# A layernorm prologue with the first x chunk loaded as two column halves and its 1/std taken from ScalarE's square root

## The chip, the cores and the metric

The kernel runs on one core of one Trainium2 chip. The metric is device time in microseconds (us) of one execution; lower is better. Each version was run several times and once under the profiler.

The engines are TensorE (PE for matmuls, PEld for weight loads), VectorE (DVE), ScalarE (ACT), GpSimd (POOL) and SyncE (SP), which issues nearly all DMAs. A chunk is 128 tokens by 1024 columns; x has 16 of them, called x0 to x15.

## The reference, cut to what matters

```python
xn = layernorm(x)                              # x: 2048 tokens x 1024
y  = x + attention(xn, wq, wk, wv, wo, beta) + B(xn)

def B(x):                                      # a token-mixing MLP
    h = layernorm(x)                           # normalised a second time
    u = gelu(einsum('bsd,sf->bdf', h, w1) + b1)
    ...
```

Only the start of branch B matters for the change. The first matmul needs h of the first 128 tokens, so it needs mean and 1/std of chunk 0. Both layernorms of B are folded into one scale, with a constant `E_H` added to the variance. Everything after the first 35 us is the same in both kernels.

## The kernel before: the parts that matter

The prologue loads x and the first columns of w1 chunk by chunk on one queue. Even chunks have their statistics on VectorE, odd ones on ScalarE. The hidden matmuls consume a chunk as soon as its h and its w1 rows are there.

```python
# consts(): order of the loads, all issued by SyncE on one queue
for kind, c0, n in (("x", 0, 1), ("x", 1, 1), ("x", 2, 1), ("w", 0, 2), ("x", 3, 1), ("x", 4, 2),
                    ("w", 2, 2), ("x", 6, 2), ("w", 4, 4), ...):
    ...
# ten matmuls on zeros: TensorE has work while x0 is on its way
for _ in range(self.N_WARM):                   # N_WARM = 10
    fw.mm(self.bank(0), self.warm[:, 0:P], self.warm[:], start=True, stop=True)

# D, d  BN_STATS on VectorE (both halves / one half; d2' is the second half of chunk 2)
# A, A' sum, then sum of squares, on ScalarE
# S     add E_H (VectorE), then pow -0.5 (POOL)
# h     scale x into h (VectorE)
NORM_ORDER = (["D0 A1 S0 d2 h0 A1' A3 S1 d2' h1"] +
              [f"S{c} d{c + 2} h{c} A{c + 1}' A{c + 3} S{c + 1} d{c + 2}' h{c + 1}" for c in range(2, 14, 2)] +
              ["S14 h14 A15' S15 C h15"])

def early_hidden(self, c0, c1, bank_groups):   # per chunk: 8 matmuls of 512 columns
    for banks in bank_groups:                  # the first half of h, then the second
        reads = self.R_w1e[c0:c1] + ... + self.R_hh[banks[0] % 2][c0:c1]
        ...
```

Each engine runs its own words of `NORM_ORDER` in that order. A word that waits for data therefore holds up the words behind it on the same engine.

## Time and profile before

| | before |
|---|---|
| median of the runs beside the change | 697.27 us (696.95 to 698.75, 6 runs) |
| span of the profiled run | 695.2 us |
| PE busy | 685.3 us, 99% of the span |
| first matmul on real data | 6.83 us |
| x0, x1, x2, first w1 piece, x4 landed | 3.57, 4.23, 5.65, 6.55, 8.82 us |

Landings here and below are the last increment of each transfer's semaphore in the trace, in us from the start of the span. "x4" is the transfer that brings chunks 4 and 5.

From the page of the kernel before (busy time by engine; then the chain that ended last, by engine):

```profile
span 695.2 us, 11228 instructions
...
PE 685.3 (99%) x4746; PEld 326.5 (47%) x4830; DVE 257.2 (37%) x581; ACT 280.2 (40%) x333; POOL 100.1 (14%) x156
...
PE 98%; issue 1%; DMA 1%; DVE 0%; SPq 0%
...
```

The kernel is bound by TensorE from end to end. A change of the prologue can pay only by moving the whole stream of matmuls. What starts that stream is seen in the timeline of VectorE (start, duration, engine, line, operation, tiles; in brackets the idle time before it and what ended it):

```profile
...
3.60 1.42 DVE L617 BATCH_NORM_STATS2 ln_st<-xin 128x6 f32<-128x512 bf16 x2 [2.35 <-DMA xin<-in_A_x_dram]
5.05 0.21 DVE L620 BATCH_NORM_AGGREGATE ln_mv<-ln_st 128x2 f32<-128x12 f32 x1
5.29 0.15 DVE L639 TENSOR_SCALAR ln_mv<-ln_mv 128x1 f32<-128x1 f32 x1
5.67 0.69 DVE L617 BATCH_NORM_STATS2 ln_st<-xin 128x6 f32<-128x512 bf16 x1 [0.23 <-DMA xin<-in_A_x_dram]
6.29 0.72 DVE L656 TENSOR_SCALAR h<-xin,ln_mv,ln_rs 128x512 bf16<-128x512 bf16 x2
...
8.85 0.69 DVE L617 BATCH_NORM_STATS2 ln_st<-xin 128x6 f32<-128x512 bf16 x1 [0.28 <-DMA xin<-in_A_x_dram]
9.46 0.53 DVE L656 TENSOR_SCALAR h<-xin,ln_mv,ln_rs 128x1024 bf16<-128x1024 bf16 x1
...
```

The POOL pow runs from 5.53 to 6.08 us, between the third and the fifth of these lines. Then h0 is held until 6.29 by the statistics of chunk 2. The line at 8.85 is chunk 4's statistics, released by the landing of x4; h2 stands right behind it. TensorE's timeline shows one stream from 6.83 us on, with no gap:

```profile
...
1.25 4.06 PE L194 MATMUL ps_all<-warm 128*128 128x512 bf16 x10 [1.25 <-DVE brow L517]
6.83 9.44 PE L194 MATMUL ps_all<-h,w1early 128*128 128x512 bf16 x42 [1.51 <-DVE h L656]
```

### The profile page before, as it was taken

The numbers are of one execution on the slowest core, as the hardware profiler recorded it, in microseconds if no ns is written. First come the engines' busy times: TensorE is split into PE (matmuls) and PEld (weight loads), VectorE is DVE, ScalarE is ACT, GpSimd is POOL, SyncE is SP. The second block draws the span as 40 slices with busy tenths as digits, with TensorE's granted clock in tenths as the row PEclk, the third lists the DMA queues.
The fourth block names the chain that finished last, engine by engine and source line by source line (L and its number), as shares of the span: only waits on it lengthen the run. The fifth ranks groups of instructions, "written<-read, shape, count | busy, mean of one in ns | idle before, by whom it ended". The sixth has DMA issues, their size and how long they took to land.

```text
span 695.2 us, 11228 instructions
## 1 busy us (share of the span) xinstructions
PE 685.3 (99%) x4746; PEld 326.5 (47%) x4830; DVE 257.2 (37%) x581; ACT 280.2 (40%) x333; POOL 100.1 (14%) x156
## 2 busy tenths in 40 slices
PE   8999999999999999999999999999999999999998
PEld 3444444444444444444444454444444444445454
DVE  6740000000011334334436455536445553434445
ACT  7622222111134444444545444454544444534440
POOL 2600000000001111211121211112121111121130
DMA  9497685226045536645263544626273544436014
GB/s 315 110 221 175 149 227 124 74 60 140 1 138 116 111 65 133 117 107 124 49 126 97 118 95 88 129 47 137 66 148 80 97 95 73 98 63 151 9 31 137
DMA packets 210537, 77.17 MB, mean 111 GB/s; under 512 B 173112, under 2 KB 202808, under 8 KB 210488
## 3 DMA queue, kind: packets, MB, share of 16 engines
q1 hardware_dynamic: 210344, 76.42, 47.9%
q8 instruction: 38, 0.62, 0.4%
q14 instruction: 11, 0.09, 0.0%
q10 hardware_dynamic: 144, 0.03, 0.0%
HBM read 59.79 MB, written 5.24 MB: 94 GB/s over the span
## 4 chain that ended last, share of the span: by engine, by line
PE 98%; issue 1%; DMA 1%; DVE 0%; SPq 0%
PE ps_all L194 98%; DMA xin<-in_A_x_dram 1%; SPq L216 0%; DVE ln_st L617 0%; DVE h L656 0%; DVE fin L1050 0%; PE ps_all L200 0%
## 5 line engine op out<-in xcount | busy, mean ns | idle before, releaser
L194 PE MATMUL ps_all<-gT,w2h 128*128 128x512 bf16 x868 | 207.8, 380 | 1.6 <-issue 0.2
L810 ACT ACTIVATE pT<-ps_all 128x512 bf16<-128x512 f32 (+1 forms) x128 | 151.4, 1235 | 76.7 <-PE ps_all L194 76.7
L194 PE MATMUL ps_all<-h,w1s 128*128 128x512 bf16 x752 | 165.1, 379 | 0.8
L805 POOL TENSOR_SCALAR_AFFINE_SELECT pT<-pT 128x512 bf16<-128x512 bf16 x128 | 83.6, 677 | 557.3 <-ACT pT L810 557.3
L194 PEld LDWEIGHTS ps_all<-gT,w2h 128*128 128x128 bf16 x896 | 83.2, 98 | 105.6 <-issue 13.8
L194 PEld LDWEIGHTS ps_all<-h,w1s 128*128 128x128 bf16 x768 | 75.1, 98 | 90.6
L844 DVE CAST ost<-ps_all 128x264 bf16<-128x264 f32 (+1 forms) x128 | 49.2, 398 | 169.4 <-PE ps_all L194 169.4
L712 ACT ACTIVATE gT<-ps_all,b1c 128x512 bf16<-128x512 f32 x56 | 37.7, 689 | 138.4 <-PE ps_all L194 132.8
L754 DVE CAST kT<-ps_all 128x512 bf16<-128x512 f32 x32 | 22.0, 687 | 176.5 <-PE ps_all L194 176.5
L194 PE MATMUL ps_all<-xnT,wk 128*128 128x512 bf16 x256 | 60.5, 379 | 0.0
L194 PE MATMUL ps_all<-xnT,wq 128*128 128x512 bf16 x256 | 60.4, 378 | 0.0
L194 PEld LDWEIGHTS ps_all<-vA,pT 128*128 128x128 bf16 x1280 | 47.7, 96 | 22.7
L194 PE MATMUL ps_all<-wv_sb,xnT 128*128 128x512 bf16 x227 | 54.0, 379 | 1.6
L738 ACT ACTIVATE qT<-ps_all 128x512 bf16<-128x512 f32 x32 | 19.1, 597 | 78.4 <-PE ps_all L194 78.4
L194 PE MATMUL ps_all<-vA,pT 128*128 128x33 bf16 x1280 | 48.6, 177 | 0.0
L950 DVE SCALAR_TENSOR_TENSOR stg<-ps_all,b2c,stg 128x512 bf16<-128x512 f32 x32 | 24.0, 750 | 61.7 <-PE ps_all L194 61.6
L757 ACT ACTIVATE etmp<-kT 128x512 bf16<-128x512 bf16 x24 | 15.1, 629 | 59.0 <-DVE kT L754 59.0
L194 PEld LDWEIGHTS ps_all<-xnT,wk 128*128 128x128 bf16 x256 | 23.8, 98 | 23.1
L194 PEld LDWEIGHTS ps_all<-wv_sb,xnT 128*128 128x128 bf16 x256 | 23.5, 97 | 23.7
L194 PEld LDWEIGHTS ps_all<-xnT,wq 128*128 128x128 bf16 x256 | 23.4, 97 | 23.2
L772 ACT ACTIVATE vA<-ps_all 128x512 bf16<-128x512 f32 x32 | 19.2, 599 | 37.2 <-PE ps_all L194 37.2
L194 PE MATMUL ps_all<-qT,kT 32*128 32x384 bf16 (+3 forms) x512 | 31.9, 299 | 0.0
(70 smaller groups left out, 419.2 us busy)
## 6 DMA issues: line engine op xcount, KB each, us to landing
w2h<-in_B_w_dram SPq DMA_DIRECT2D x32, 448.0 KB, 4.8
w1s<-in_B_w_dram SPq DMA_DIRECT2D x12, 1024.0 KB, 5.7
wq<-in_A_wq_dram SPq DMA_DIRECT2D x32, 256.0 KB, 4.2
wk<-in_A_wk_dram SPq DMA_DIRECT2D x32, 256.0 KB, 5.0
stg<-in_A_x_dram SPq DMA_DIRECT2D x16, 256.0 KB, 2.9
out_dram<-stg SPq DMA_DIRECT2D x16, 256.0 KB, 2.0
xin<-in_A_x_dram SPq DMA_DIRECT2D x2, 1024.0 KB, 10.5
wv_sb<-in_A_wv_dram SPq DMA_DIRECT2D x2, 1024.0 KB, 8.7
```

What stands on the lines that cost most here:

```text
L194: ins = self.nc.tensor.matmul(*args, **kwargs)
L712: fw.op("act", lambda e: e.activation(self.gT[:, fc, half * 512:(half + 1) * 512], self.bank(b), ACT.Gelu_apprx_tanh, bias=self.b1c[:, fc: ...
L738: fw.op("act", lambda e: e.activation(self.qT[k][:], self.bank(b), ACT.Copy), reads=[self.R_bank[b]], writes=[self.R_qT[k]])
L754: fw.op("dve", lambda e: e.tensor_copy(self.kT[k][:], self.bank(b)), reads=[self.R_bank[b]], writes=[self.R_kT[k]])
L757: fw.op("act", lambda e: e.activation(self.etmp[1][:], self.kT[k][:], ACT.Exp), reads=[self.R_kT[k]], writes=[self.R_etmp[1]])
L772: fw.op("act", lambda e: e.activation(self.vA[i][:, c, :, 0:D_HEAD], self.bank(b).rearrange("p (h d) -> p h d", d=D_HEAD), ACT.Copy), read ...
L805: fw.op("pool", lambda e: e.affine_select(d, d, pattern=[[0, 4], [1, P]], compare_op=ALU.is_ge, fill=0.0, base=0, channel_multiplier=-1), ...
L810: self.fw.op("act", lambda e: e.activation(dst, src, ACT.Exp, scale=SCALE), reads=R_src, writes=R_dst)
L844: fw.op("dve", lambda e: e.tensor_copy(dst, self.ps[:, b, 0:n * VW]), reads=[self.R_bank[b]], writes=[self.R_ost[o][qb]])
L950: fw.op("dve", lambda e: e.scalar_tensor_tensor(dst, self.bank(b), self.b2c[:, c:c + 1], dst, op0=ALU.add, op1=ALU.add), reads=[self.R_ban ...
```

## The change

The intent is to have h of chunk 0 sooner. The first x chunk arrives as two column halves, so that the first half's statistics start while the second is still on its way. Its 1/std no longer takes the way over POOL: ScalarE takes the square root, with `E_H` as its bias, and VectorE the reciprocal. The Sqrt table is loaded at the start in place of Gelu's, and Gelu's at the end of the prologue. Chunk 2's first statistics move behind h0. The diff, cut to its core:

```diff
+        self.load_table(ACT.Sqrt)              # was: one Gelu activation
 ...
     def load_x(self, c0, n):
+        if c0 == 0:
+            for h, R in enumerate((self.R_xin[0], self.R_x0b)):
+                self.fw.dma(self.xin[:, 0, 512 * h:512 * h + 512], self.x_d[:, 0, 512 * h:512 * h + 512], writes=[R])
+            return
 ...
-    NORM_ORDER = (["D0 A1 S0 d2 h0 A1' A3 S1 d2' h1"] +
+    NORM_ORDER = (["D0 A1 Q0 h0 A1' A3 d2 S1 d2' h1 V0"] +
 ...
-                  ["S14 h14 A15' S15 C h15"])
+                  ["S14 h14 A15' G S15 C h15"])
 ...
+    def rstd_sqrt(self, c):                    # word Q
+        rs = self.ln_rs[:, c, 1:2]
+        fw.op("act", lambda e: e.activation(rs, self.ln_mv[:, c, 1:2], ACT.Sqrt, bias=self.e_h[:]), ...)
+        fw.op("dve", lambda e: e.reciprocal(rs, rs), ...)
```

`V0` adds `E_H` to chunk 0's stored variance later, for the other layernorm; `G` loads Gelu's table.

More of the change, by code (lines that the diff above doesn't have):

```diff
@@ L395, in alloc @@
         self.expo = a.take("expo", [P, N_TCH], F32)
+        self.e_h = a.take("e_h", [P, 1], F32)
         self.ln_sm = a.take("ln_sm", [P, N_TCH, 1], F32)
@@ L430, in alloc @@
         self.R_xin = [Res(f"xin{c}") for c in range(N_TCH)]
+        self.R_x0b = Res("x0b")
         self.R_junk, self.R_warm = Res("junk"), Res("warm")
@@ L521, in consts @@
         self.R_w1e = [Res(f"w1e{c}") for c in range(N_TCH)]
-        fw.op("act", lambda e: e.activation(self.junk[:, 0:1], self.warm[:, 0:1], ACT.Gelu_apprx_tanh),
-              reads=[self.R_warm], writes=[self.R_junk])
-        for kind, c0, n in (("x", 0, 1), ("x", 1, 1), ("x", 2, 1), ("w", 0, 2), ("x", 3, 1), ("x", 4, 2), ("w", 2, 2), ("x", 6, 2),
-                            ("w", 4, 4), ("x", 8, 4), ("w", 8, 4), ("x", 12, 4), ("w", 12, 4)):
+        self.load_table(ACT.Sqrt)
+        for kind, c0, n in (("x", 0, 1), ("x", 1, 1), ("x", 2, 1), ("w", 0, 2), ("x", 3, 1), ("x", 4, 2), ("w", 2, 2),
+                            ("x", 6, 2), ("w", 4, 4), ("x", 8, 4), ("w", 8, 4), ("x", 12, 4), ("w", 12, 4)):
             if kind == "x":
@@ L539, in consts @@
         fw.op("pool", lambda e: e.memset(self.expo[:], -0.5), writes=[self.R_expo])
+        fw.op("pool", lambda e: e.memset(self.e_h[:], E_H), reads=[self.R_expo], writes=[self.R_expo])
         fw.op("pool", lambda e: e.memset(self.ident[:], 0.0), writes=[self.R_ident])
@@ L547, in consts, with load_table @@
                 fw.mm(self.bank(0), self.warm[:, 0:P], self.warm[:], start=True, stop=True)
+    def load_table(self, func):
+        self.fw.op("act", lambda e: e.activation(self.junk[:, 0:1], self.warm[:, 0:1], func), reads=[self.R_warm],
+                   writes=[self.R_junk])
     def bias_columns(self):
@@ L604, in norm_and_first_hidden @@
                 self.rstd(c)
+            elif kind == "Q":
+                self.rstd_sqrt(c)
+            elif kind == "V":
+                self.add_e_h(c)
+            elif kind == "G":
+                self.load_table(ACT.Gelu_apprx_tanh)
             else:
@@ L617, in stats_dve @@
             fw.op("dve", lambda e: e.bn_stats(st[:, 6 * h:6 * h + 6], src[:, 512 * h:512 * h + 512]),
-                  reads=[self.R_xin[c]], writes=[R])
+                  reads=[self.R_x0b if c == 0 and h else self.R_xin[c]], writes=[R])
         if halves[-1]:
@@ L637, in rstd, with add_e_h @@
         fw = self.fw
-        R, var, rs = self.R_st[c], self.ln_mv[:, c, 1:2], self.ln_rs[:, c, 1:2]
-        fw.op("dve", lambda e: e.tensor_scalar(var, self.ln_sm[:, c, :] if c % 2 else var, 1.0 / D_MODEL if c % 2 else 1.0,
-                                               E_H, op0=ALU.mult, op1=ALU.add), reads=[R], writes=[R])
-        fw.op("pool", lambda e: e.tensor_tensor(rs, var, self.expo[:, 0:1], op=ALU.pow), reads=[R, self.R_expo],
-              writes=[self.R_rs[c]])
+        self.add_e_h(c)
+        fw.op("pool", lambda e: e.tensor_tensor(self.ln_rs[:, c, 1:2], self.ln_mv[:, c, 1:2], self.expo[:, 0:1],
+                                                op=ALU.pow), reads=[self.R_st[c], self.R_expo], writes=[self.R_rs[c]])
+    def add_e_h(self, c):
+        var = self.ln_mv[:, c, 1:2]
+        self.fw.op("dve", lambda e: e.tensor_scalar(var, self.ln_sm[:, c, :] if c % 2 else var,
+                                                    1.0 / D_MODEL if c % 2 else 1.0, E_H, op0=ALU.mult, op1=ALU.add),
+                   reads=[self.R_st[c]], writes=[self.R_st[c]])
+    def rstd_sqrt(self, c):
+        fw = self.fw
+        rs = self.ln_rs[:, c, 1:2]
+        fw.op("act", lambda e: e.activation(rs, self.ln_mv[:, c, 1:2], ACT.Sqrt, bias=self.e_h[:]),
+              reads=[self.R_st[c], self.R_expo], writes=[self.R_rs[c]])
+        fw.op("dve", lambda e: e.reciprocal(rs, rs), reads=[self.R_rs[c]], writes=[self.R_rs[c]])
     def rstd_first(self):
```

## The prediction

> **What bounds the kernel.** TensorE. On the page PE is busy 99% of the 695.2 us span; the chain that ended last is 98% PE and, in order of time, one PE piece after another from 6.83 us on. Only what moves the whole matmul stream counts: its start, or a chunk of h or w1 that comes too late for it.
>
> **What sets 6.83 (timeline, DMA landings).** x0 lands 3.57; two BN_STATS (0.69 each), aggregate to 5.26, E_H add to 5.45, POOL pow 5.53 to 6.08. Then chunk 2's statistics (x2 landed 5.65) hold VectorE until 6.29. The first half of h0 ends 6.68, PE starts 6.83. Close behind are other limits:
> - the first w1 piece lands 6.55: PE no earlier than about 6.65;
> - a chunk takes PE 8 x 0.2157 = 1.73 us. h1's first half ends 8.19, wanted 8.55: slack 0.22 after a hop of 0.147. h2 ends 9.99, wanted 10.28: slack 0.14. h2 sits behind chunk 4's statistics, which wait for x4 (landed 8.82).
>
> So a perfect h0 is worth at most 0.14 us unless h2 comes earlier too.
>
> **What the change does.**
> - Takes E_H add and pow from chunk 0's chain, 0.82 us with hops; adds Sqrt and reciprocal. The Trainium skill ("ScalarE: Activation LUTs", What ACT_TABLE_LOAD costs) gives 186 ns + 0.833 ns an element, 93 ns more for a pointer operand; the trace agrees (1.057 us for 1024 columns, 1.148 with a pointer bias). So Sqrt about 0.28, reciprocal about 0.15 (as the 128x1 add), hops 0.15: 0.6. Saves 0.2.
> - First half lands about 0.3 earlier (estimate: half of x0's packets), so the aggregate ends near 4.9. But Sqrt stands behind A1 (1.15 us on ScalarE), which ended 5.40 and waits for x1.
> - Each later DMA issue comes 0.45 later, and 256 packets of 1 KB (about 52 ns) replace 128 of 2 KB (about 80): 16 x 52 - 8 x 80 = 0.2 us more on each DMA engine. I expect x1, x2, the first w1 and x4 to land 0.1 to 0.25 later.
> - Chunk 2's first statistics move behind h0: h0 is unblocked (0.17), but 0.69 us of VectorE comes between h0 and chunk 1's 1/std. V0 adds 0.15 before h2.
> - Table load at start: 1.28, as before. Gelu's load moves to about 26 us, where ScalarE is idle: free. I expect no extra loads for Identity and Square.
>
> **Sum.** Aggregate 4.9; A1 ends about 5.6; Sqrt 5.9; reciprocal 6.1; h0 from 6.2; h side ready for PE about 6.75, w1 side 6.85. h1's first half then ends about 8.7 (was 8.19), ready 8.85: a start of 7.1 in PE's terms; h2 ready about 10.45: 7.0. The stream moves from 6.83 to about 7.0: nothing gained at its first matmul, a stall of 0.1 to 0.4 us before chunk 1. Nothing later changes. Net +0.15 us.
>
> Predicted 697.5 us, 8 times in 10 within 696.6 to 698.3 (before: 697.14 to 697.45; most of the width is run noise). Faster by over 2%: 0.01; within 2%: 0.98; slower: 0.01.
>
> **What would show it.** First BN_STATS near 3.3, not 3.60; Sqrt starting as A1's accumulator read ends, not when the aggregate ends; first real matmul between 6.6 and 6.95; a gap in the matmuls about 1.7 us later, released by h1; x1 and w1 landing 0.1 to 0.25 later; the chain from 50 us on the same.
>
> **What would make it wrong.** Landings not delayed, so that A1 ends by 5.3: up to 0.2 us gain. Sqrt's table lacking Square or Identity: loads of 1.28 us between statistics, +1 to 3 us. Semaphore slots of later DMAs shift by one, which might add a wait.

## The result and the profile after

| | before | after |
|---|---|---|
| median, same rounds | 697.27 us (6 runs) | 698.14 us (697.61 to 699.39, 6 runs) |
| ratio | | 1.0012, 95% interval 0.9999 to 1.0025: the same at 2% |
| span of the profiled run | 695.2 us | 695.9 us |
| first real matmul | 6.83 us | 6.88 us |
| last matmul of chunk 1 starts | 10.06 us | 10.48 us |
| first matmul of chunk 2 starts | 10.28 us | 10.97 us |

Ratios are the mean time of one kernel's runs over that of the other's of the same rounds, so not quite the ratio of the medians.

The two profiled runs differ by 0.7 us, and all of it is there when chunk 2 begins: 10.97 - 10.28 = 0.70. (This holds for every trace below: from chunk 2's first matmul to the end of the span it is 684.85 to 684.89 us in all of them, but for e14's 685.06, where a stall follows later. So the loss of a trace is read from the start of chunk 2.) The timeline of ScalarE after the change:

```profile
...
4.75 1.06 ACT L643 ACTIVATE junk<-xin 128x1024 bf16<-128x1024 bf16 x1 [2.45 <-DMA xin<-in_A_x_dram]
5.71 0.19 ACT L643 ACTIVATION_READ_ACCUMULATOR junk<-xin 128x1 f32 x1
5.81 0.28 ACT L667 ACTIVATE ln_rs<-ln_mv,e_h 128x1 f32<-128x1 f32 x1
...
```

VectorE after the change:

```profile
...
3.13 1.50 DVE L633 BATCH_NORM_STATS2 ln_st<-xin 128x6 f32<-128x512 bf16 x2 [1.88 <-DMA xin<-in_A_x_dram]
4.66 0.21 DVE L636 BATCH_NORM_AGGREGATE ln_mv<-ln_st 128x2 f32<-128x12 f32 x1
6.12 0.16 DVE L669 RECIPROCAL ln_rs<-ln_rs 128x1 f32<-128x1 f32 x1 [1.25 <-ACT ln_rs L667]
6.32 0.74 DVE L683 TENSOR_SCALAR h<-xin,ln_mv,ln_rs 128x512 bf16<-128x512 bf16 x2
...
9.69 0.69 DVE L633 BATCH_NORM_STATS2 ln_st<-xin 128x6 f32<-128x512 bf16 x1 [0.34 <-DMA xin<-in_A_x_dram]
10.30 0.53 DVE L683 TENSOR_SCALAR h<-xin,ln_mv,ln_rs 128x1024 bf16<-128x1024 bf16 x1
...
```

The aggregate ends at 4.87 us, 0.39 us sooner than before. Then VectorE waits 1.25 us for the square root. The root stands behind A1 on ScalarE (the first two ACT lines), and A1 waited for x1, which landed at 4.73 us instead of 4.23. So h0 starts at 6.32, where it was 6.29. In all eight traces that have the square root, h0 starts 1.58 to 1.63 us after x1's landing: chunk 0 now depends on chunk 1's transfer, and an earlier aggregate cannot help. (The root ahead of A1 on ScalarE was not run.) TensorE now has a visible gap:

```profile
...
1.25 4.14 PE L194 MATMUL ps_all<-warm 128*128 128x512 bf16 x10 [1.25 <-DVE brow L519]
6.88 1.89 PE L194 MATMUL ps_all<-h,w1early 128*128 128x512 bf16 x8 [1.49 <-DVE h L683]
8.96 7.14 PE L194 MATMUL ps_all<-h,w1early 128*128 128x512 bf16 x31 [0.20 <-DVE h L683]
```

The starts of matmuls 8 and 9 are 8.385 and 8.962 us. Less the normal distance of 0.216, that is a stall of 0.36 us before chunk 1. A second one of 0.28 us (10.483 to 10.974) lies before chunk 2 and is too short to break the line. The chain of waits names its cause: the transfer of x4, issued at 3.65 us, landed at 9.66.

```profile
...
3.65 6.01 DMA xin<-in_A_x_dram
9.66 0.02 issue
9.69 0.36 DVE ln_st L633
10.05 0.25 issue
10.30 0.53 DVE h L683
...
10.97 5.12 PE ps_all L194 x23
...
```

Before, x4 landed at 8.82 us. So the changed kernel had what it wanted, an earlier aggregate, but with later landings.

### The profile page after: what moved, and what is told of

The parts are those of the page before. It is cut to its first block, busy times and chain, and to the rows that moved or that the text cites. A ratio compares the mean times of both kernels' runs of the same rounds, so it can differ in the third digit from the quotient of the medians.

```text
span 695.9 us, 11234 instructions
## 1 busy us (share of the span) xinstructions
PE 685.7 (99%) x4746; PEld 326.2 (47%) x4830; DVE 257.5 (37%) x582; ACT 281.9 (41%) x336; POOL 99.9 (14%) x156
## 4 chain that ended last, share of the span: by engine, by line
PE 97%; DMA 1%; issue 1%; SPq 0%; DVE 0%
PE ps_all L194 97%; DMA xin<-in_A_x_dram 1%; SPq L216 0%; DVE h L683 0%; DVE ln_st L633 0%; DVE fin L1077 0%; PE ps_all L200 0%; DVE ln_mv L660 0%
```

## The experiments

Theory A: the split's effect on the landings of the transfers behind it costs the time. Variants of it: A1, the additional issue on the queue is the cause; A2, the smaller packets are. Rivals: B, the late x4 was chance; C, Sqrt and the new order cost the time. A second trace of the changed kernel brought up D: some executions start with TensorE at half speed, whatever the kernel. (Theories A1 and A2 have nothing to do with the word `A1` of the order; "theory A1" is the theory, "A1 ends" is chunk 1's statistics on ScalarE.) Every run gave the reference's result.

Landings and first matmuls of all traces (us):

```
                          x1    x2    w1    x4     first real   spacing of the
                                                   matmul       first matmuls
before                    4.23  5.65  6.55   8.82   6.83         0.216
before, second trace      4.17  5.92  6.60   8.83   7.09         0.216
after                     4.73  5.72  6.39   9.66   6.88         0.216
after, second trace       5.49  6.23  6.86   9.55   7.63         0.427
e1  halves only           5.63  6.32  6.99   9.98   7.50         0.427
e2  Sqrt and order only   4.31  6.33  7.05   9.14   7.10         0.216
e5  row halves            4.92  5.79  7.33  10.98   7.38         0.427
e6  second half by ACT    4.20  5.79  6.78   8.83   6.83         0.427
e9  after, 14 warm-ups    5.22  5.90  6.58  10.59   7.37         0.216
e10 before, 14 warm-ups   4.19  4.86  6.35   8.65   6.75         0.216
e11 e6, 14 warm-ups       4.26  6.07  6.75   8.78   7.08         0.216
e12 e2, 14 warm-ups       4.12  6.25  7.26   9.24   7.30         0.216
e13 e1, 14 warm-ups       5.49  6.19  6.85  10.15   7.37         0.216
e14 e9, d4 behind h2      5.50  6.18  6.86  10.31   7.65         0.216
```

### Both kernels once more

No edit; a second trace of each.

> The kernel before, unchanged, for a second trace: how much the landings move from run to run. Both theories: real matmuls from about 6.8 us without a gap, time within 0.1% of 697.3 us. Theory A (the split itself delays the landings) expects x4 to land again near 8.8 us (within 0.3). Theory B (the late x4 of the changed kernel was chance of one run) expects x4 anywhere between 8.8 and 9.7.

Measured: 697.08 us median (696.73 to 700.56, 6 runs), ratio 0.9998 (0.9981 to 1.0016). x1 and x4 landed within 0.06 us of the first trace. The start missed the expectation: x2 came 0.27 us later, h0 waited for it, and the first matmul was at 7.09.

> The changed kernel, unchanged, for a second trace. Theory A (split delays the landings): x1 near 4.7, x4 near 9.6 us, two gaps in the matmuls again (before chunk 1 about 0.35 us, before chunk 2 about 0.27 us), time +0.5 to +0.9 us on the kernel before. Theory B (late x4 was chance): the gap before chunk 1 stays, that before chunk 2 shrinks below 0.1, time +0.2 to +0.4 us.

Measured: 698.70 us median (697.87 to 700.67, 6 runs), ratio 1.0015 (0.9999 to 1.0030). The late landings came again, x1 even at 5.49 us. That speaks against B. The two gaps did not come, for a reason that nobody had expected:

```profile
...
1.25 4.45 PE L194 MATMUL ps_all<-warm 128*128 128x512 bf16 x10 [1.25 <-DVE brow L519]
7.63 8.60 PE L194 MATMUL ps_all<-h,w1early 128*128 128x512 bf16 x26 [1.93 <-DVE h L683]
```

In 8.60 us there are 26 matmuls; the kernel before has 42 in 9.44 us. The first 13 or so real matmuls start 0.427 us apart in place of 0.216, just as the warm-up matmuls did: TensorE ran at half speed until 13.4 us, where the trace records its first full clock. What their distances have over 0.216 us sums to 2.8 us. The slow matmuls hide the two stalls, since h is ready in time for them. This gave theory D.

### e1: only the split

```diff
 # the kernel before, and
+        if c0 == 0: (two column halves of x0 on SyncE's queue, as in the change)
```

> The kernel before with only the x0 load split into column halves; POOL pow and the old order stay. Theory A (the split's landings cost the time): x1 near 4.7, x2 near 5.7, x4 near 9.6 us; h0 waits for chunk 2's statistics and starts near 6.35; first matmul near 6.9; no gap before chunk 1 (h1's first half ready near 8.5), a gap of about 0.6 us before chunk 2; time +0.6 to +0.8 us, nearly the whole loss. Rival C (order and Sqrt cost the time): first matmul about 6.8, time within 0.2 us of the kernel before.

Measured: 699.07 us median (697.55 to 699.11, 5 runs), ratio 1.0011 (0.9998 to 1.0024), nearly the ratio of the whole change. x1 came at 5.63 and x4 at 9.98. The first matmul was later than expected, 7.50, and this trace, too, began at half speed (three of the five runs took 699.07 us or more); so the ratio says nothing of the split's size, and e13 repeats it.

### e2: all but the split

```diff
 # the changed kernel, but
-        if c0 == 0: (two column halves)
```

> The changed kernel with x0 loaded whole by one DMA; Sqrt, reciprocal, V0 and the new order stay. Theory A (the split's landings cost the time): x1 near 4.2 and x4 near 8.8 as before; A1 ends 5.4, Sqrt 5.4 to 5.7, h0 from about 5.95; first matmul near 6.65, set by the first w1 piece; a gap of about 0.3 us before chunk 1, none or under 0.1 before chunk 2; time within 0.2 us of the kernel before. Rival C (order and Sqrt cost the time): +0.5 us or more with normal landings.

Measured: 697.44 us median (697.22 to 698.64, 5 runs), ratio 1.0001 (0.9988 to 1.0014). Rival C falls at the size of the loss. Without the split A1 ends at 5.48, the root at 5.67, and h0 starts at 5.90 us, 0.39 sooner than before. It bought nothing: the first w1 piece landed at 7.05 us in this run, and the first matmul waited for it until 7.10. The expected gap before chunk 1 did not come, since the matmuls started late.

### e5 and e6: the issue or the packets?

e5 loads x0 as two row halves: two issues, but packets of 2 KB as before.

```diff
 # the kernel before, and
+                self.fw.dma(self.xin[64 * h:64 * h + 64, 0, :], self.x_d[64 * h:64 * h + 64, 0, :], writes=[R])
```

> The kernel before with x0 loaded as two row halves (64 partitions each) on the same queue: two issues as in the change, but x0 keeps its 128 packets of 2 KB. Theory A1 (the extra issue, 0.46 us, lets the queue run dry before x1): x1 lands at 4.6 or later and starts with slow packets (0.5 us and more) near 2.9 us, x4 lands near 9.6. Rival A2 (the packets of 1 KB are the cost): x1 lands within 0.15 of 4.23, x4 within 0.3 of 8.82, first matmul near 6.85, no gap.

Measured: 699.31 us median (698.21 to 699.79, 5 runs), ratio 1.0025 (1.0012 to 1.0038). x1 at 4.92 and x4 at 10.98 us, with packets of full size: A1's forecast. One thing differs from the plan: the two row issues took 0.57 us each, the column ones 0.40, so x1's issue was put off by 0.8 us in place of 0.46. So this is A1's forecast in kind, not a test of its size. The run also had a third kind of start. Full clock was granted at 4.02 us, withdrawn at 7.43 and granted again at 10.85. The view by stretches shows the granted clock (third column from the right; the one before last is the DMA engines' busy share; before a trace's first recorded change the column reads 1.00 whatever the clock, as in the second trace of the change, and there the spacing of the matmuls tells):

```profile
...
4.10:7.40 3.30, 0.85 (x5) 0.22 (x4) 3.01 (x8) 2.39 (x4) 0.55 (x1) 1.00 1.00 297
7.50:10.80 3.30, 3.30 (x9) 1.11 (x9) 1.52 (x6) 2.39 (x4) 1.10 (x2) 0.50 1.00 348
10.90:14.00 3.10, 3.10 (x16) 1.38 (x15) 2.97 (x8) 2.88 (x5) 0.95 (x2) 1.00 1.06 387
...
```

The record also has each run's mean granted clock. One window at half speed makes it 1 - 0.5 x 3.41/697, or 0.998, and four of e5's five runs read 0.997 or 0.998: its time is not to be compared. So do two runs of the changed kernel with ten warm-up matmuls, one of e1 and three of the kernel before.

e6 keeps the change and its packets of 1 KB, but ScalarE issues the second half at the same time as SyncE issues the first.

```diff
-                self.fw.dma(..., writes=[R])
+                self.fw.dma(..., writes=[R], issuer=("sp", "act")[h])   # Sqrt's table load stands behind it
```

> The changed kernel with the second half of x0 issued from ScalarE's queue at the same time as the first (Sqrt's table load behind it), so SP issues x1, x2, w1 as early as in the kernel before; packets of x0 stay 1 KB. Theory A1 (late issue of x1 is the cause): x1 lands 4.2 to 4.4, x4 near 8.9, Sqrt ends before 5.8, first matmul before 6.85, second gap (before chunk 2) under 0.1, time within 0.3 us of the kernel before. Rival A2 (1 KB packets): x1 4.6 or later, as in the change, time +0.6 us or more.

Measured: 697.25 us median (696.98 to 698.76, 5 runs), ratio 1.0000 (0.9987 to 1.0014). x1 at 4.20 and x4 at 8.83 us: the landings of the kernel before. So 1 KB packets are not the cost (A2 falls), and the additional issue ahead of x1 on one queue is (A1). e6 takes a transfer off the queue and brings x1's issue forward, both at once; a later x1 alone was not run, so which of the two counts stays open. Whether a gap before chunk 2 is left can't be seen here, since the run began at half speed; e11, the same kernel with 14 warm-up matmuls, has none. The stretch from 3.0 to 3.5 us shows the difference in what the DMA engines moved (last column, GB/s). The kernel before:

```profile
...
3.00:3.50 0.50, 0.50 (x3) 0.23 (x2) 0.00 (x0) 0.00 (x0) 0.00 (x0) 1.00 1.02 389
...
```

The changed kernel:

```profile
...
3.00:3.50 0.50, 0.50 (x3) 0.22 (x2) 0.37 (x1) 0.00 (x0) 0.00 (x0) 1.00 0.91 166
...
```

e6:

```profile
...
3.00:3.50 0.50, 0.50 (x3) 0.23 (x2) 0.02 (x1) 0.00 (x0) 0.00 (x0) 1.00 1.06 404
...
```

In the changed kernel x0's first half has landed by then (3.10) and its second is about to (3.54), and many of x1's first packets, from 2.84 us on, took 0.3 to 0.8 us each, as x0's first ones did in the kernel before (up to 0.6); the usual packet of 2 KB takes 0.084. This looks like a queue that ran dry and started anew. That reading is argued from the packets' times, not tested. The Trainium skill ("DMA: Bandwidth & Descriptors", Issuing engines are not separate DMA queues) says that the DMA engines are shared whoever issues, and that a second issuing engine only saves the sequencer's time for the issue, "which is usually small relative to the DMA itself". The sharing agrees: in e6 x0's first half landed at 3.46 us, against 3.10, with the second half's packets beside it. The time saved mattered here: an issue is 0.46 us from start to start, a sixth of the 2.76 us from x0's issue to its landing, but most of the 0.66 us by which x1 landed after x0 before.

e6's profiled run also began at half speed, and took 698.63 us; its three quickest took 696.98, 697.06 and 697.25.

### e9 and e10: the cold start

```diff
-    N_WARM = 10
+    N_WARM = 14
```

> The changed kernel with 14 warm-up matmuls in place of 10. The second trace of the changed kernel ran its first 13 real matmuls at 0.427 us each and lost 2.7 us by that. Theory D (TensorE's full clock is granted only in some executions before the ten warm-up matmuls end, whatever the kernel): with 14 no execution starts with matmuls of 0.427, the runs of 698.5 us and more disappear, all lie between 697.4 and 698.3, and the loss of 0.5 to 0.9 us on the fast mode of the kernel before stays. Rival: the slow runs have another cause, and some stay over 698.5.

> The kernel before with 14 warm-up matmuls. Theory D: no run over 697.9 us (5 of 23 runs with ten were over 698.4), all between 696.7 and 697.7, first real matmul near 6.9, mean 0.3 to 0.5 us below the kernel before. Rival: the slow runs have another cause, about one in five stays over 698.4.

Measured, in the same rounds: the changed kernel 698.13 us median (697.92 to 698.51, 5 runs, so the top is 0.2 over the forecast and 0.01 over the rival's line, but it is the traced run, and that did not start at half speed), the kernel before 696.94 (696.85 to 697.23, 5 runs), ratios to the unaltered kernel before 1.0010 (0.9998 to 1.0023) and 0.9993 (0.9981 to 1.0006). Neither trace starts at half speed. With ten warm-up matmuls the kernel before gave 41 runs in all, and 11 of them took 698.4 us or more. With 14, the three versions with x1 and x4 near their old landings (e10, e11, e12) gave 15 runs, the longest of 697.96 us; and all 30 runs with 14 read a mean clock of 1.000. Of the eight traces with ten, the four that began (or fell back) at half speed are those of runs of 698.6 us and more; the four others took 696.9 to 697.6. So D holds. With the blur gone, the change costs 698.19 - 697.01 = 1.18 us (means of five), and the two sets of runs do not overlap. That is more than the expected 0.5 to 0.9 us; against the eight quick runs of the unaltered kernel in these rounds (mean 697.25) it is 0.94. e9's timeline has both stalls, 0.36 us before chunk 1 and 0.71 before chunk 2:

```profile
...
7.37 1.89 PE L194 MATMUL ps_all<-h,w1early 128*128 128x512 bf16 x8 [0.95 <-DVE h L683]
9.45 1.90 PE L194 MATMUL ps_all<-h,w1early 128*128 128x512 bf16 x8 [0.20 <-DVE h L683]
11.90 4.26 PE L194 MATMUL ps_all<-h,w1early 128*128 128x512 bf16 x19 [0.55 <-DVE ln_mv L660]
```

The Trainium skill ("TensorE: Matmul & The Clock Gate", What's actually happening) tells of a free-running window of 3413 ns over which the matmuls' activity is judged. The traces agree: e5's three changes of the clock are 3.41 us apart. When the first full clock comes differs by run: 4.0 us (e5), 7.1 (e12), and 13.4 in the second trace of the change.

The traces show more. Count back in steps of 3.41 us from each recorded change, and see how much of each stretch held matmuls. The stretches that ended in the full clock held them for 81% (e5), 92% (e14), 95% (before, second trace) or all of their length; those that did not, for 55, 75 and 68% (the change, second trace), 67% (e11) and 73% (e12). The full clock was withdrawn after a stretch of 28% (e5) and kept after one of 43% (before, second trace). From these figures, an estimate: ten warm-up matmuls at half speed last 4.45 us. If the stretches begin by chance, such a warm-up fills one of them to 75% in 80 of 100 runs, and to 81% in 68. From 5.1 us (for 75%) or 5.5 us (for 81%) on it always does, and 14 matmuls at half speed last 6.0. That fits the 11 slow runs of 41, three of which had the full clock withdrawn, and none with 14.

TensorE's timeline for the kernel before with 14:

```profile
...
1.25 4.76 PE L194 MATMUL ps_all<-warm 128*128 128x512 bf16 x14 [1.25 <-DVE brow L517]
6.75 9.44 PE L194 MATMUL ps_all<-h,w1early 128*128 128x512 bf16 x42 [0.73 <-DVE h L656]
```

### e11, e12, e13: the parts again, with 14 warm-up matmuls

e11 is e6, e12 is e2 and e13 is e1, each with `N_WARM = 14`.

> The ScalarE-queue version of the change with 14 warm-up matmuls. The same version with ten had x1 at 4.20 and runs of 696.98 to 697.25 apart from two of 698.6 and more. Theory A1 plus D: no run over 697.6, mean within 0.25 us of 697.0 (the kernel before with 14 warm-ups): with the landings restored, Sqrt, the reciprocal and the earlier half are worth nothing measurable, because the first w1 piece (lands 6.3 to 6.8), h1 and h2 all bind within 0.15 us of the old start. Rival E (Sqrt was the gain and only the landings hid it): 696.7 or less.

> Sqrt, reciprocal and the new order with x0 whole, and 14 warm-up matmuls, so that the cold start does not blur it. Theory A1: mean within 0.25 us of 697.0, no gap over 0.3 before chunk 1. Rival C (order and Sqrt cost part of the loss): 697.4 or more with x1 near 4.2.

> The kernel before with only the split of x0 on the one queue, and 14 warm-up matmuls. Theory A1: x1 4.7 to 5.7, x4 9.5 to 10.7; mean 697.8 to 698.6, that is 0.8 us or more over 697.0 and within 0.4 us of the changed kernel with 14 warm-ups (698.19). Rival C (the split alone is harmless): 697.4 or less.

Measured, all in the same rounds:

| | mean of 5 | range | ratio to the kernel before (10 warm-ups) |
|---|---|---|---|
| e11, second half by ScalarE | 697.21 us | 696.83 to 697.96 | 0.9984 (0.9971 to 0.9996) |
| e12, no split | 697.29 us | 696.79 to 697.51 | 0.9984 (0.9971 to 0.9998) |
| e13, only the split | 697.85 us | 697.58 to 698.09 | 0.9993 (0.9980 to 1.0005) |

With the split alone the time is 697.85 - 697.29 = 0.56 us over e12's, without overlap. The two differ in the square root and the order too; e10, which differs from e13 by the split alone, is 0.84 us quicker, but ran on another chip. Both are less than the 1.18 of the whole change. In the traces the size of the loss follows x4's landing: chunk 2 starts 1.31 us after it in e9, in e13 and in the first trace of the change alike, with the new order and the old, and x4 landed at 10.59 us in e9 and at 10.15 in e13. Those are single traces, so what Sqrt and the order add when the landings are late stays open. e13's stalls are 0.21 us before chunk 1 and 0.42 before chunk 2, the second again behind x4's statistics:

```profile
...
10.17 0.70 DVE L622 BATCH_NORM_STATS2 ln_st<-xin 128x6 f32<-128x512 bf16 x1 [0.54 <-DMA xin<-in_A_x_dram]
10.78 0.53 DVE L661 TENSOR_SCALAR h<-xin,ln_mv,ln_rs 128x1024 bf16<-128x1024 bf16 x1
...
```

e11 (one run 0.36 us over its forecast, 697.96) and e12 (mean 0.04 over) have h0 at 5.85 and 5.75 us, 0.4 to 0.5 sooner than the kernel before, and are not quicker than e10 (697.01 us, but on another chip). So where x1 and x4 land as before, Sqrt and the earlier half gain nothing that these runs can see. In both traces the warm-up ran at half speed almost to its end, and the real matmuls follow it without a gap. In e12 w1 landed at 7.26 us anyway; in e11, with w1 there at 6.75, the warm-up itself may have held the first real matmul (7.08 us) by up to 0.3 us. The favourable ratios of this table owe much to the kernel before, of whose nine runs five took 698.4 us or more there.

### e14: h2 no longer behind chunk 4's statistics

```diff
 # the changed kernel with N_WARM = 14, and for chunk 2
-   S2 d4 h2 A3' A5 S3 d4' h3
+   S2 h2 A3' A5 d4 S3 d4' h3
```

> The changed kernel with 14 warm-up matmuls and one move on VectorE: the statistics of chunk 4 stand behind the scaling of h2, so that h2 no longer waits for x4. If x4 was what held h2 (the second gap of the changed kernel, 0.28 to 0.71 us): the gap before chunk 2 is under 0.1, that before chunk 1 stays near 0.36, mean 697.5 to 698.0, 0.2 to 0.7 under the changed kernel with 14 warm-ups (698.19), unless the delayed x3 brings a new gap before chunk 3. Rival: the gap before chunk 2 stays, h2 was late for another reason.

Measured: 697.62 us median, mean 697.83 (697.54 to 698.39, 5 runs). x4 landed at 10.31 us (e9: 10.59), but the gap before chunk 2 is 0.09 us in place of e9's 0.71, too short to break the line:

```profile
...
7.65 1.89 PE L194 MATMUL ps_all<-h,w1early 128*128 128x512 bf16 x8 [1.68 <-DVE h L684]
9.73 6.48 PE L194 MATMUL ps_all<-h,w1early 128*128 128x512 bf16 x28 [0.20 <-DVE h L684]
```

The gap before chunk 1 stays at 0.36, and a new one of 0.17 us came before chunk 3, probably since the moved statistics now stand in h3's way. So the wait for x4 was what held h2. The mean is 0.36 us under e9's, but e9 ran in other rounds, on another chip, so the time alone proves little; the gaps do.

## Why the prediction was right or wrong

The measured time lies in the predicted range, and the class, the same at 2%, was right. The direction was right as well, though the interval of the ratio just reaches 1. That the time lies in the range is owed to the width that was put in for run noise, and so in part to luck: the forecast loss of 0.15 us was 0.70 in the traces and 1.18 with the slow starts removed. The delays of the landings were sized too small.

- **TensorE's start and its two close limits:** right, as far as tested. e2, e11 and e12 had h0 0.4 to 0.5 us sooner and no gain; what held them was the first w1 piece, or the longer warm-up (e2's first matmul came 0.05 us after w1's landing, like e6's). The slack of 0.14 us of h2 was not tested by itself. The forecast start of 6.6 to 6.95 held in the first trace (6.88) and not in the second (7.63).
- **Sqrt and reciprocal:** right. They took 0.28 and 0.16 us, and from the root's start to h0 it is 0.51 us against an estimate of 0.6. The skill's page on ScalarE ("ScalarE: Activation LUTs", What ACT_TABLE_LOAD costs) gave the 0.28.
- **Sqrt waits for A1, not for the aggregate:** right. It started at 5.81 us, when A1's read was under way; the aggregate had ended at 4.87.
- **Tables:** right. There are two loads in the whole changed prologue, at 0.81 and 25.86 us; Identity and Square ran under Sqrt's table.
- **"I expect x1, x2, the first w1 and x4 to land 0.1 to 0.25 later":** this is the term that was mis-sized. x1 came 0.50 and 1.26 us later in the two traces, x4 0.84 and 0.73. The w1 piece came once 0.16 earlier, once 0.31 later. The reason given was wrong too. The 0.2 us for smaller packets is not there: e6 has them and x1 lands at 4.20, and the usual packets of the trace take 46 and 84 ns in place of 52 and 80, which makes 16 x 46 - 8 x 84 = 64 ns. The cost is the place of x1's issue in the queue: 0.46 us later in all traces with the column split on one queue, and x1 0.50 to 1.40 later.
- **Stalls:** the one before chunk 1, "0.1 to 0.4 us", was 0.36. The prediction had h2 ready for a start of 7.0 in TensorE's terms. It was 10.97 - 2 x 1.726 = 7.52, so chunk 2 set the loss: a second stall, from x4's landing. This is why the sum was 0.15 us and the trace says 0.70, and with the clock's chance removed 1.18 (e9 against e10).
- **Not foreseen at all:** the half-speed starts. They happen in the kernel before too, by their times in 11 of 41 runs. They put 1.5 us on a run like e6's (698.63 against 697.10, the mean of its three quickest) and made the second trace of the change 698.8 us long where the first was 695.9.

What stays open: why x1's first packets and later x3's and x4's are slow once x1 is issued late (packets of 0.5 to 1.7 us between 5.5 and 7.6 us in the traces with the split on one queue); whether the change makes the half-speed start more frequent (6 of its 12 runs with ten warm-up matmuls took 698.6 us or more, too few to tell); and whether Sqrt and the order are worth some tenths either way, which two chips' runs can't tell.

The experiments point to one version that comes out below both kernels: the kernel before with 14 warm-up matmuls (e10). Its median is 696.94 us against 697.25 of the unaltered one and 698.13 of the change with 14, and none of its runs was slow; its ratio to the kernel before, 0.9993, is within the noise of five runs.

## What to carry to other kernels

Before an early transfer is split to start its consumer sooner, count the transfers behind it on that queue: an issue costs 0.46 us there, and where the next transfer's consumer is as close to the critical path as the first's, the split moves the wait instead of removing it. Look at how much slack the second and third chunk have, not only at the first; here the slack read from the first trace left 0.14 us to win. And when times fall into two groups, look at the spacing of the first matmuls before anything else is compared. By the estimate above, the warm-up had to be long enough to fill one of the clock's windows wherever the window began.

## What the Trainium skill lacked or had wrong

- "TensorE: Matmul & The Clock Gate" (Why this matters for your kernels) advises to warm up with at least 4 us of matmuls. Here 3.7 to 4.5 us of warm-up (ten matmuls; the three traces that then began at half speed had 4.45) left 11 of 41 runs of the kernel before slow, and three of eight traces not at full clock before the real matmuls. The first full clock came 2.8 (e5), 5.9 (e12) and 12.1 us (the change, second trace) after the first warm-up matmul. The page lacks how full a window must be: here 75% did not bring the full clock and 81% did, so that a safe warm-up lasts some 5.5 us (the estimate under e9 and e10).
- The same page says an idle window returns the clock to half. In e5 the clock was withdrawn at 7.43 us although the stretch from 4.1 to 7.4 held 0.85 us of matmuls; the window need not be empty.
- "DMA: Bandwidth & Descriptors" (Issuing engines are not separate DMA queues) calls the issue time usually small relative to the DMA. Here it was 0.40 to 0.43 us for each of the first four transfers (0.57 and 0.58 for the first three of e5), where a 256 KB transfer landed 0.66 us after the one before it; moving one issue to ScalarE brought x1 from 4.73 back to 4.20 us.
- "ScalarE: Activation LUTs" gives a drain of about 1380 ns with every switch to a different set. At the start of these traces the load took 1.28 us and the next activation began 0.01 us later; at the switch from Sqrt's table to Gelu's (25.86 us) ScalarE's last work had ended 0.02 us before the load, and the next began 0.01 us after it. No drain is seen there. Its table doesn't say whether Square is in Sqrt's set; the trace shows that it runs there without a further load.
